# A planner's figures for loads and four ranks are changed, and the order of a retention + gated MLP kernel is planned anew

## The chip, the cores and the metric

The kernel runs on one core of a Trainium2 chip. The metric is the device time of one execution in microseconds (us); lower is better. Every time here comes from runs of this kernel or from the trace of one profiled execution.

## The reference, cut to what matters

Inputs: `q`, `k`, `v` of shape (4 batches, 8 heads, 768 tokens, 64), all fp32, and the weights `w_val`, `w_out` (512x512) and `conv_w` (5x512) of a gated layer.

```python
for t in range(S):                                   # retention, per batch and head
    state = gamma * state + outer(k[t], v[t])
    y[t]  = scale * q[t] @ state
x    = y as (batch, 768, 512)
gate = sigmoid(causal depthwise conv of x, 5 taps)
out  = (gate * (x @ w_val)) @ w_out
```

## The kernel before

The tokens are cut into 6 chunks of 128; a chunk of one batch is a unit `g` (24 units, `g = 4*chunk + batch`). A unit's q, k (transposed), v and k (natural) lie in a 1 MiB tile `att`; there are 4 such buffers, so unit g+4 overwrites unit g. The weights come as 8 tiles `wst` of 0.5 MiB and are converted on chip: w0 to w3 are `w_val`, w4 to w7 `w_out`. fp32 accuracy in the large matmuls comes from splitting both operands into a high and a low part (`xh`/`xl`, `wvh`/`wvl`, `gvh`/`gvl`, `woh`/`wol`) and adding three products.

Steps, with the line on which they show in the profile of the kernel before (in the changed kernel every one of these lines is 10 further down):

- First chunk, units 0 to 3: `first_scores` (L379, PE, writes `sy`), `first_mask` (L411, DVE, `sy` to `u`), `first_y` (L456, PE, writes `ye`), `evac` (L519, DVE, to `x`), `round_x` (L529, ACT, `xh`), `rest_x` (L534, POOL, `xl`), and `first_state` (L423, PE, writes `z_ps`). A POOL step `decay` (L355) scales a unit's k or v in place ahead of its state. `first_pos` (L498) makes a table from `pos`; `y` of unit 0 can only be evacuated behind it.
- Later units: a `head` for unit 4 (scores L366 and half of the state, L423), then one `visit` per unit: `y_scores` (L439), state (L423), a small ACT copy `turn`, `y_state` (L439) and the scores of the next unit (L366). Visits consist of 64x64 matmuls, each of which the profile shows as two.
- Per chunk and group m of 128 channels: 4 conv taps on DVE (L610) behind a first on ACT (L608), a sigmoid, and a val tile of 12 matmuls of 128x512 (L625); then per batch an out tile of 12 such matmuls (L659), a copy on ACT (L670) and a store.
- `filler` (L689): dummy matmuls that the planner puts into idle time of PE ahead of the first val matmul; `warm_up` is the same at the start.

The order on each engine isn't written by hand: `plan` simulates the five engines with the cost of each step, always takes the free step with the lowest rank (worked out backwards from the due times of the PE steps), and records the instructions in that order. The due times come from the string `WORK` (p: pos, s: first scores, y: first y, z: first state, h: head, v: visit, w: load and convert a weight, V: val tile, O: out tile) and from the list `LOADS`, the order of the first loads on SP's queue. In `LOADS` q is q and transposed k of a unit (0.5 MiB), v and k the other two (0.25 MiB each), a is q, k and v together (0.75 MiB), t the small table (68 KB), w a weight tile (0.5 MiB). Each engine runs its own instructions strictly in the recorded order.

Of the kernel before, what the change touches and what calls it, by code (L numbers as in the profile page):

```python
# [33 lines left out]
INTO, OUT_OF = 0.3, 0.134  # L34
COLD, WARM_AT = 1.85, 5.0
FIRST_PAGE, PAGE, FETCH, CROWDED = 94, 127.5, 3.0, 2.9
FIRST_BYTE, PER_MB = 4.1, 2.7
TABLES = (5.2, 9.3)

TIMES = {  # L40
# [6 lines left out]
}  # L47
FILL, FILLED = 0.46, 0.55
SEEN = {"DVE": 0.035, "ACT": 0.035, "POOL": 0.08, "PE": 0.08}


class Slot:
# [26 lines left out]
def plan(steps, filler, last, into):  # L79
# [5 lines left out]
    steps = sorted(steps, key=lambda s: s.due)  # L85
# [47 lines left out]
    while ends:  # L133
        t = ends.pop()
        for s in before[t.index]:
            if s.engine == "PE" or not hasattr(s, "rank"):
                s.rank = min(getattr(s, "rank", s.due if s.engine == "PE" else 1e9), 1e9)
            lag = s.cost + SEEN.get(t.engine, 0.0) if t in s.then else 0.0
            s.rank = min(s.rank, t.rank - lag) if s.engine != "DMA" else s.due
            left[s.index] -= 1  # L140
            if not left[s.index]:
                ends.append(s)
    clock, free = {}, {}

    def offer(s):
# [48 lines left out]
    def offered(e):  # L194
        return free[e] if e != "PE" or held is None else [s for s in free[e] if s is held]

    def done(s, end):
# [7 lines left out]
        for t in s.then:  # L205
            if t.engine == s.engine and not t.other:
                t.own = max(t.own, clock["PE"] if t.engine == "PE" else end + 0.03)
            else:
                t.ready = max(t.ready, end + SEEN.get(t.engine, 0.0))
            t.waits.discard(s.index)  # L210
# [3 lines left out]
    while any(free.values()):  # L214
# [5 lines left out]
        s = min(  # L220
            (s for s in offered(e) if max(s.ready, s.own if s.engine == e else 0.0) <= start),
            key=lambda s: (s.rank, s.index),
        )
# [26 lines left out]
        if s.turn:  # L250

            t, e = s.turn, s.turn.engine
# [10 lines left out]
def tile_retention_gated_mlp(  # L263
# [9 lines left out]
    nc = tc.nc  # L273
# [20 lines left out]
    small_sb = const.tile([P, small.shape[1]], F32, name="small_sb")  # L294
# [23 lines left out]
    steps = []  # L318

    def at(due, engine, cost, reads, writes, fn, *args):  # L320
        steps.append(Step(due, engine, cost, list(reads), list(writes), fn, args))
        return steps[-1]
# [371 lines left out]
    def first_sigmoid():  # L694
# [6 lines left out]


    CONV_LEAD, CHUNK = 7.0, 3.4
    LOADS = (("q", 0), ("t", 0), ("k", 0), ("v", 0), ("w", 0), ("a", 1), ("w", 1), ("a", 2), ("a", 3), ("k", 1), ("w", 2), ("k", 2), ("k", 3), ("w", 3))


    WORK = (
        "spysysszyyzzzVwwVwwhvVVOOvvOvOVvVvVVOvOvVVO"
        "vvVOvVvOVVOvOvVVOvvOVOvVOOvvvVVOVOOVVOVOOOO"
    )  # L710

    first_val = []
# [4 lines left out]
    def load_part_at(due, g, first, last):  # L717

        keys = [("att", g % LB, k) for k, part in (("qk", 0), ("vk", 2), ("kn", 3)) if first <= part < last]
        at(due, "DMA", 0.4, [], keys, load, g, slice(first, last)).mb = 0.25 * (last - first)  # L720
# [101 lines left out]
    def load_w_at(t, n):  # L822
        at(t, "DMA", 0.4, [], [wsts[n]], load_w, n).mb = 0.5
# [59 lines left out]
    at(0.2, "DVE", 0.25, [], [xbufs[0]] + [("x", 0, i) for i in range(B)], new_x, 0)  # L883
    for p, (kind, n) in enumerate(LOADS):
        t = 0.1 * p
        if kind == "t":
            at(t, "DMA", 0.4, [], ["small"], get, small_sb, small, nc.sync).mb = 0.2
        elif kind in "aqvk":
            load_part_at(t, n, *{"a": (0, 3), "q": (0, 2), "v": (2, 3), "k": (3, 4)}[kind])
        else:  # L890
            load_w_at(t, n)
    for x in range(2):
        for k, (engine, cost) in enumerate((("DVE", (0.42, 0.35)), ("ACT", (0.25, 0.2)))):
# [4 lines left out]
            )  # L898
    early = [n for kind, n in LOADS if kind == "w"]
    for n in ["cw"] + early:  # L900
        convert(5.5, n)

    t, whole = 6.0, {}
# [3 lines left out]
    for what in WORK:  # L907
# [7 lines left out]
        elif what == "s":  # L915
            t = max(t, 6.0 + CHUNK * i)
# [29 lines left out]
    with tc.manual_schedule():  # L946
        for step in plan(steps, filler, first_val[0], ("ye", "sc")):
            step.fn(*step.args)
# [93 lines left out]
```

## Time and profile before

| | |
|---|---|
| median of 3 runs | 210.98 us (210.53 to 211.2) |
| the profiled execution | 210.8 us |
| its span, first to last instruction | 209.0 us |
| granted TensorE clock | 1.00 |
| PE, DVE, ACT, POOL busy | 96%, 59%, 53%, 51% of the span |

In a row of the timeline stand the start, the length, the engine (PE is the matmul side of TensorE, SPq and ACTq are queues that issue DMAs), the line, the operation with what it writes and reads, the count, and in brackets the idle time of the engine before it and what ended that. Rows are merged runs of like instructions; matmuls are pipelined, so a row's length overlaps the next row, and differences of starts are used for durations. In a row of the windows view stand the stretch, its length, the busy time and number of instructions of each engine named, the clock, the DMA engines' busy share and their GB/s.

### The profile page before, as it was taken

The numbers are of one execution on the slowest core, as the hardware profiler recorded it, in microseconds if no ns is written. First come the engines' busy times: TensorE is split into PE (matmuls) and PEld (weight loads), VectorE is DVE, ScalarE is ACT, GpSimd is POOL, SyncE is SP. The second block draws the span as 40 slices with busy tenths as digits, with TensorE's granted clock in tenths as the row PEclk, the third lists the DMA queues.
The fourth block names the chain that finished last, engine by engine and source line by source line (L and its number), as shares of the span: only waits on it lengthen the run. The fifth ranks groups of instructions, "written<-read, shape, count | busy, mean of one in ns | idle before, by whom it ended". The sixth has DMA issues, their size and how long they took to land.

```text
span 209.0 us, 7837 instructions
## 1 busy us (share of the span) xinstructions
PE 199.7 (96%) x3502; PEld 159.3 (76%) x3502; DVE 123.5 (59%) x189; ACT 110.2 (53%) x237; POOL 105.9 (51%) x93
## 2 busy tenths in 40 slices
PE   8967898999999999999999999999999999999994
PEld 3647676788888888788887888788787788878783
DVE  1586999952399814899129992227796259921100
ACT  3584687774667434685338654146364445413121
POOL 0189999999824582536627324526142353204200
PEclk9999999999999999999999999999999999999999
DMA  6999994557555508527275138348111100120122
GB/s 213 411 408 412 418 413 167 204 172 274 167 204 204 204 3 279 226 94 258 109 256 204 50 108 270 130 161 299 53 50 53 56 0 0 50 103 0 50 100 102
DMA packets 9253, 36.24 MB, mean 173 GB/s; under 512 B 1154, under 2 KB 1538, under 8 KB 6660
## 3 DMA queue, kind: packets, MB, share of 16 engines
q1 hardware_dynamic: 5472, 29.43, 37.7%
q10 hardware_dynamic: 3748, 6.32, 8.2%
q8 instruction: 27, 0.44, 0.9%
q14 instruction: 6, 0.05, 0.1%
HBM read 29.46 MB, written 6.29 MB: 171 GB/s over the span
## 4 chain that ended last, share of the span: by engine, by line
PE 89%; DMA 7%; issue 1%; DVE 1%; SPq 0%; ACT 0%; ACTq 0%
PE mm L659 33%; PE mm L625 33%; PE sy L439 11%; PE z_ps L423 5%; DMA att<-in_att_dram 5%; PE sy L366 5%; DMA cw_raw<-in_conv_w_dram 2%; PE sy L689 1%; PE sy L379 0%; DVE u L411 0%; PE ye L456 0%; DVE x L519 0%; SPq L342 0%; ACT gate L670 0%; SPq L545 0%
## 5 line engine op out<-in xcount | busy, mean ns | idle before, releaser
L610 DVE SCALAR_TENSOR_TENSOR acc<-x,cw_sb,acc 128x512 f32<-128x512 f32 x96 | 66.8, 750 | 2.7 <-ACT acc L608 2.1
L534 POOL TENSOR_TENSOR xl<-x,xh 128x512 fp32r<-128x512 f32 x24 | 30.9, 1288 | 44.0 <-ACT xh L529 44.0
L651 POOL TENSOR_TENSOR gvl<-gate,gvh 128x512 fp32r<-128x512 f32 x24 | 30.9, 1289 | 30.6 <-ACT gvh L647 30.6
L659 PE MATMUL mm<-woh,gvl 128*128 128x512 f32 (+1 forms) x100 | 38.7, 396 | 0.0
L659 PE MATMUL mm<-woh,gvh 128*128 128x512 f32 (+1 forms) x100 | 38.2, 390 | 0.0
L659 PE MATMUL mm<-wol,gvh 128*128 128x512 f32 (+1 forms) x100 | 37.9, 387 | 0.0
L625 PE MATMUL mm<-xl,wvh 128*128 128x512 f32 x96 | 34.4, 399 | 0.0
L625 PE MATMUL mm<-xh,wvh 128*128 128x512 f32 x96 | 32.0, 399 | 0.0
L355 POOL TENSOR_TENSOR att<-att,small_sb 128x512 f32<-128x512 f32 x24 | 25.1, 1049 | 12.4 <-DMA att<-in_att_dram 12.4
L640 DVE TENSOR_TENSOR gate<-mm,gate 128x512 f32<-128x512 f32 x24 | 16.5, 688 | 20.5 <-PE mm L625 18.1
L625 PE MATMUL mm<-xh,wvl 128*128 128x512 f32 x96 | 27.0, 397 | 0.0
L647 ACT CAST gvh<-gate 128x512 fp32r<-128x512 f32 x24 | 14.9, 619 | 22.1 <-DVE gate L640 22.0
L388 DVE TENSOR_TENSOR u<-sy,small_sb 128x512 f32<-128x512 f32 x20 | 13.7, 687 | 21.6 <-PE sy L366 21.6
L519 DVE TENSOR_TENSOR x<-sy,dec 128x512 f32<-128x512 f32 x20 | 13.7, 683 | 17.3 <-PE sy L366 12.5
L659 PEld LDWEIGHTS mm<-woh,gvl 128*128 128x128 f32 x100 | 18.7, 188 | 4.7 <-POOL gvl L651 0.5
L670 ACT COPY o_sb<-mm 128x512 f32<-128x512 f32 x23 | 13.5, 586 | 16.5 <-PE mm L659 16.1
L659 PEld LDWEIGHTS mm<-woh,gvh 128*128 128x128 f32 x100 | 18.7, 188 | 4.4 <-ACT o_sb L670 0.2
L617 ACT ACTIVATE gate<-acc 128x512 f32<-128x512 f32 x24 | 14.4, 600 | 14.1 <-DVE acc L610 7.8
L529 ACT CAST xh<-x 128x512 fp32r<-128x512 f32 x24 | 14.9, 619 | 13.0 <-DVE x L519 12.1
L659 PEld LDWEIGHTS mm<-wol,gvh 128*128 128x128 f32 x100 | 18.7, 188 | 3.8
L625 PEld LDWEIGHTS mm<-xl,wvh 128*128 128x128 f32 x96 | 18.0, 188 | 4.4
L625 PEld LDWEIGHTS mm<-xh,wvl 128*128 128x128 f32 x96 | 17.9, 188 | 4.3
(52 smaller groups left out, 248.2 us busy)
## 6 DMA issues: line engine op xcount, KB each, us to landing
att<-in_att_dram SPq DMA_DIRECT2D x20, 1024.0 KB, 5.3
out_dram<-o_sb ACTq DMA_DIRECT2D x23, 256.0 KB, 2.2
wst<-in_w_dram SPq DMA_DIRECT2D x8, 512.0 KB, 8.7
att<-in_att_dram SPq DMA_DIRECT2D x3, 768.0 KB, 7.2
att<-in_att_dram SPq DMA_DIRECT2D x5, 256.0 KB, 10.4
att<-in_att_dram SPq DMA_DIRECT2D x1, 512.0 KB, 3.6
out_dram<-gate ACTq DMA_DIRECT2D x2, 128.0 KB, 1.7
small_sb<-in_small_dram SPq DMA_DIRECT2D x1, 68.0 KB, 3.5
```

Source lines behind the costliest of these rows:

```text
L355: nc.gpsimd.tensor_tensor(v, v, vd_sb[:, c, :].unsqueeze(2).broadcast_to([P, 8, HALF]), op=ALU.mult)
L388: nc.vector.tensor_tensor(us[g], sy[:, :, 0:256].rearrange("p x (a t) -> p x a t", t=HALF), tri_sb.unsqueeze(1).unsqueeze(1).broadcast_to( ...
L439: nc.tensor.matmul(sy[cols, h, off:off + HALF], lhsT=lhsT, rhs=rhs, start=start, stop=True, skip_group_check=True,)
L529: nc.scalar.copy(xh[n][:, :, b], xs[n][:, :, b, HALO:])
L534: nc.gpsimd.tensor_tensor(xl[n][:, :, b], xs[n][:, :, b, HALO:], xh[n][:, :, b].bitcast(F32), op=ALU.subtract)
L610: nc.vector.scalar_tensor_tensor(acc, x[:, :, k:k + P], cw_sb[:, m, k:k + 1], acc, op0=ALU.mult, op1=ALU.add,)
L617: nc.scalar.activation(gate[n, m], accs.pop((n, m)), AF.Sigmoid)
L625: nc.tensor.matmul(vps[n, m], lhsT=w[:, m, ct * P:(ct + 1) * P], rhs=xx[n][:, ct].rearrange("p b t -> p (b t)"), start=(i == 0), stop=(i = ...
L640: nc.vector.tensor_tensor(gv, vps.pop((n, m)), gv, op=ALU.mult)
L647: nc.scalar.copy(gvs[n, m][0], gate[n, m])
L651: engine.tensor_tensor(gvl, gate.pop((n, m)), gvh.bitcast(F32), op=ALU.subtract)
L659: nc.tensor.matmul(ops[n, b, cs.start][:, 0:cs.stop - cs.start], lhsT=gg[:, b * P:(b + 1) * P], rhs=w[:, ct, cs], start=(i == 0), stop=(i ...
```

## The change

Two figures of the planner for loads are changed (`FIRST_BYTE` and `PER_MB`, used for when a load lands), the size that it books for the small table goes from 0.2 to 0.13 MB, four kinds of steps get a number added to their rank (`LATER`: the split of unit 1 of the first chunk, the first state of unit 3, the sums of weights 3 and the rounding of weight 6), and `LOADS` and `WORK` are other sequences of the same steps. No step is added to the arithmetic or taken from it; the fillers, which `plan` places by itself, go from 11 calls to 13.

```diff
-FIRST_BYTE, PER_MB = 4.1, 2.7
+FIRST_BYTE, PER_MB = 3.0, 2.65
+LATER = {
+    ("rest_x", 0, 1): 1.47,
+    ("first_state", 3): -2.94,
...
+    for s in steps:
+        s.rank += LATER.get((s.fn.__name__, *(a for a in s.args if isinstance(a, int))), 0.0)
...
-    LOADS = (("q", 0), ("t", 0), ("k", 0), ("v", 0), ("w", 0), ("a", 1), ("w", 1), ("a", 2), ("a", 3), ("k", 1), ("w", 2), ("k", 2), ("k", 3), ("w", 3))
+    LOADS = (("q", 0), ("k", 0), ("t", 0), ("v", 0), ("a", 1), ("k", 1), ("w", 0), ("k", 2), ("k", 3), ("w", 1), ("a", 2), ("w", 2), ("a", 3), ("w", 3))
...
-        "spysysszyyzzzVwwVwwhvVVOOvvOvOVvVvVVOvOvVVO"
+        "sspyysyzszhyVVwzzwvVwvwVOOOvvvOVvvVVVvOVvOvV"
...
-            at(t, "DMA", 0.4, [], ["small"], get, small_sb, small, nc.sync).mb = 0.2
+            at(t, "DMA", 0.4, [], ["small"], get, small_sb, small, nc.sync).mb = 0.13
```

**SP's queue, the first loads.** A row is one load; 128x1024 is 0.5 MiB, x512 0.25, x1536 0.75, x2048 1 MiB. Before, from the second load on (`att_102` is unit 0, `att_120`, `att_126` and `att_129` are units 1, 2 and 3, `att_206` is unit 4):

```order
L342 DMA att_102<-in_att_dram 128x512 x2
L545 DMA wst_117<-in_w64_dram 128x1024
L342 DMA att_120<-in_att_dram 128x1536
L545 DMA wst_123<-in_w64_dram 128x1024
L342 DMA att_126<-in_att_dram 128x1536
L342 DMA att_129<-in_att_dram 128x1536
L342 DMA att_120<-in_att_dram 128x512
L545 DMA wst_133<-in_w64_dram 128x1024
L342 DMA att_126<-in_att_dram 128x512
L342 DMA att_129<-in_att_dram 128x512
L545 DMA wst_154<-in_w64_dram 128x1024
L342 DMA att_206<-in_att_dram 128x2048
```

After, where `att_116`, `att_125`, `att_128` and `att_245` are units 1, 2, 3 and 4:

```order
L352 DMA att_103<-in_att_dram 128x512
L352 DMA att_116<-in_att_dram 128x1536
L352 DMA att_116<-in_att_dram 128x512
L555 DMA wst_122<-in_w64_dram 128x1024
L352 DMA att_125<-in_att_dram 128x512
L352 DMA att_128<-in_att_dram 128x512
L555 DMA wst_131<-in_w64_dram 128x1024
L352 DMA att_125<-in_att_dram 128x1536
L555 DMA wst_150<-in_w64_dram 128x1024
L352 DMA att_128<-in_att_dram 128x1536
L555 DMA wst_157<-in_w64_dram 128x1024
L352 DMA att_245<-in_att_dram 128x2048
```

The natural k of units 1, 2 and 3 now comes ahead of q, k, v of units 2 and 3, and so does the third weight tile ahead of those of unit 3; the sum of bytes up to unit 4 is the same. On ACT's own queue, which loads the conv weights `cw_raw` and `pos`, the load of the sigmoid's table now stands ahead of these two instead of behind them.

**PE, from the y of unit 3 to the first val tile.** Before (`z_ps<-att_120`, `att_126`, `att_129` are the first states of units 1, 2, 3; `sy<-const` are filler calls):

```order
L456 MATMUL ye_96<-u_336,att_129 64x64 x8
L689 MATMUL sy_95<-const-float32-0.0 128x128 x2
L423 MATMUL z_ps_94<-att_120 64x64 x16
L689 MATMUL sy_95<-const-float32-0.0 128x128 x4
L423 MATMUL z_ps_94<-att_126 64x64 x16
L625 MATMUL mm_428<-xh_217,wvh_89 128x512 x4
L423 MATMUL z_ps_94<-att_129 64x64 x16
L625 MATMUL mm_428<-xh_217,wvl_90 128x512 x4
```

After (`sy<-att_245` and `z_ps<-att_245` are the head of unit 4):

```order
L466 MATMUL ye_96<-u_365,att_128 64x64 x8
L699 MATMUL sy_95<-const-float32-0.0 128x128 x6
L376 MATMUL sy_95<-att_245 64x64 x16
L433 MATMUL z_ps_94<-att_245 64x64 x8
L635 MATMUL mm_447<-xh_272,wvh_89 128x512 x4
L635 MATMUL mm_447<-xh_272,wvl_90 128x512 x4
```

Three fillers and the head now stand ahead of the first val matmul; the first state of unit 1 has moved up to the loads' first stretch, and those of units 2 and 3 behind it. On POOL, which feeds this, stood before:

```order
L355 TENSOR_TENSOR att_120<-att_120,small_sb_86 128x512
L534 TENSOR_TENSOR xl_242<-x_104,xh_217 128x4x128
L355 TENSOR_TENSOR att_126<-att_126,small_sb_86 128x512
L355 TENSOR_TENSOR att_129<-att_129,small_sb_86 128x512
L534 TENSOR_TENSOR xl_242<-x_104,xh_217 128x4x128
L582 TENSOR_TENSOR top_341<-top_341,up_342 128x512
```

and stands now:

```order
L544 TENSOR_TENSOR xl_280<-x_105,xh_272 128x4x128
L365 TENSOR_TENSOR att_245<-att_245,small_sb_86 128x512
L592 TENSOR_TENSOR top_362<-top_362,up_363 128x512
L544 TENSOR_TENSOR xl_280<-x_105,xh_272 128x4x128
L365 TENSOR_TENSOR att_282<-att_282,small_sb_86 128x512
```

The decays of units 1 to 3 (`att_120`, `att_126`, `att_129` before) have moved to the front of POOL's order; now the decay of unit 4 and the sum of the third weight tile stand ahead of the split `xl` of unit 3, which is the last `xl` row of each list.

**PE, ahead of the first visit.** Before, head and first visit (`u_559`) with 12 val matmuls between them:

```order
L366 MATMUL sy_95<-att_206 64x64 x16
L423 MATMUL z_ps_94<-att_206 64x64 x8
L625 MATMUL mm_536<-xh_217,wvh_89 128x512 x4
L625 MATMUL mm_536<-xh_217,wvl_90 128x512 x4
L625 MATMUL mm_536<-xl_242,wvh_89 128x512
L625 MATMUL mm_561<-xh_217,wvh_89 128x512
L625 MATMUL mm_536<-xl_242,wvh_89 128x512
L625 MATMUL mm_561<-xh_217,wvh_89 128x512
L439 MATMUL sy_95<-u_559,att_206 64x64 x16
```

After, with the first states of units 2 and 3 (`att_125`, `att_128`) and three val matmuls ahead of the first visit (`u_480`):

```order
L635 MATMUL mm_465<-xh_272,wvl_90 128x512 x4
L635 MATMUL mm_465<-xl_280,wvh_89 128x512
L433 MATMUL z_ps_94<-att_125 64x64 x16
L433 MATMUL z_ps_94<-att_128 64x64 x16
L635 MATMUL mm_465<-xl_280,wvh_89 128x512 x3
L449 MATMUL sy_95<-u_480,att_245 64x64 x16
```

Small matmuls now stand closer together there: three val matmuls lie between the states and the visit instead of twelve between head and visit. On all of PE the changed order has 22 separate runs of large matmuls, the order before 23.

More of the change, by code (lines that the diff above doesn't have):

```diff
@@ L49 @@
 SEEN = {"DVE": 0.035, "ACT": 0.035, "POOL": 0.08, "PE": 0.08}
+LATER = {
+    ("rest_x", 0, 1): 1.47,
+    ("first_state", 3): -2.94,
+    ("cv_sum", 3): 0.77,
+    ("cv_round", 6): 3.83,
+}
 class Slot:
@@ L703, in tile_retention_gated_mlp @@
     CONV_LEAD, CHUNK = 7.0, 3.4
-    LOADS = (("q", 0), ("t", 0), ("k", 0), ("v", 0), ("w", 0), ("a", 1), ("w", 1), ("a", 2), ("a", 3), ("k", 1), ("w", 2), ("k", 2), ("k", 3), ("w", 3))
+    LOADS = (("q", 0), ("k", 0), ("t", 0), ("v", 0), ("a", 1), ("k", 1), ("w", 0), ("k", 2), ("k", 3), ("w", 1), ("a", 2), ("w", 2), ("a", 3), ("w", 3))
     WORK = (
-        "spysysszyyzzzVwwVwwhvVVOOvvOvOVvVvVVOvOvVVO"
-        "vvVOvVvOVVOvOvVVOvvOVOvVOOvvvVVOVOOVVOVOOOO"
+        "sspyysyzszhyVVwzzwvVwvwVOOOvvvOVvvVVVvOVOvV"
+        "vVvVvOvOVOOvVVVvvOOVOVvVvvOvVOOVVOOOVOVOOOO"
     )
```

## The prediction

> **What bounds the kernel now.** I read the page first, then PE's time by stretches.
>
> ```profile
> PE 199.7 (96%) x3502; PEld 159.3 (76%) x3502; DVE 123.5 (59%) x189; ACT 110.2 (53%) x237; POOL 105.9 (51%) x93
> q8 instruction: 27, 0.44, 0.9%
> ```
>
> ```profile
> 40.00:80.00 40.00, 40.00 (x881) 1.00 0.47 168
> 80.00:120.00 40.00, 40.00 (x765) 1.00 0.52 185
> ```
>
> From 40 us on PE has no gap; DVE, ACT and POOL have half of their time free. Both orders hold the same 588 large matmuls and the same visits, so whatever the change does to the middle moves nothing unless it opens a gap there. The time is decided by how soon the first val matmul starts, what is left to do by then, and the gaps around the first visit. PE's timeline there:
>
> ```profile
> 15.75 1.00 PE L379 MATMUL sy<-att 64*64 64x128 f32 x32 [0.76 <-DMA att<-in_att_dram]
> 18.43 0.90 PE L456 MATMUL ye<-u,att 64*64 64x128 f32 x32 [1.01 <-DVE x L519]
> 19.25 0.71 PE L689 MATMUL sy<-const-float32-0.0 128*128 128x128 f32 x4
> 22.12 0.71 PE L689 MATMUL sy<-const-float32-0.0 128*128 128x128 f32 x5 [1.00 <-issue]
> 22.77 0.69 PE L423 MATMUL z_ps<-att 64*64 64x64 f32 x32
> 23.39 1.20 PE L625 MATMUL mm<-xh,wvh 128*128 128x512 f32 x4
> 24.52 0.69 PE L423 MATMUL z_ps<-att 64*64 64x64 f32 x32
> 25.15 1.20 PE L625 MATMUL mm<-xh,wvl 128*128 128x512 f32 x4
> 30.01 0.69 PE L366 MATMUL sy<-att 64*64 64x64 f32 x32
> 30.52 0.41 PE L423 MATMUL z_ps<-att 64*64 64x64 f32 x16
> 30.87 1.20 PE L625 MATMUL mm<-xh,wvh 128*128 128x512 f32 x4
> 33.86 0.69 PE L439 MATMUL sy<-u,att 64*64 64x64 f32 x32
> 36.29 0.68 PE L366 MATMUL sy<-att 64*64 64x64 f32 x27 [0.66 <-issue]
> ```
>
> The scores of unit 3 wait for their load (15.75), the first val matmul starts at 23.39, the first visit at 33.86. Two waits are put down to "issue", to no other engine and no tensor's load. They stand 255 matmuls apart by the order (254 recorded, first row below). The page counts 27 packets on the instruction queue for 3502 matmuls and as many weight loads, 130 matmuls a packet, so two packets lie between the waits. I read them as PE's own code arriving late.
>
> ```profile
> 22.12:36.28 14.16, 13.51 (x254) 1.00 0.82 333
> 136.57:140.34 3.77, 3.77 (x142) 1.00 0.44 148
> 65.72:67.78 2.06, 2.06 (x130) 1.00 0.41 167
> 33.86:36.90 3.04, 2.38 (x130) 1.00 0.16 35
> 5.20:31.00 25.80, 21.41 (x480) 16.48 (x480) 20.10 (x32) 17.70 (x38) 20.99 (x19) 1.00 1.02 412
> ```
>
> If a block is asked for when the one before it begins, the block that arrived at 36.29 was asked for 127 matmuls after 22.12, at the head's state (30.5): 5.8 us, while loads filled the DMA engines (share 1.02 until 31). In a calm stretch 142 matmuls ran in 3.77 us without a wait, so a block then takes 3.8 us at most. The first visit cost 3.04 us against 2.06 for a common one: 1.0 lost.
>
> **The start, part by part.** *Loads.* SP's queue has new places, but through unit 3's q, k, v it now carries as many bytes (5.57 MiB) as it did through the natural k of unit 3, and through unit 4 the same 7.07 MiB. Those two landed at 7.6 + 11.3 = 18.9 and 11.0 + 11.7 = 22.7:
>
> ```profile
> L342 SPq DMA_DIRECT2D att<-in_att_dram x1: 328/328/328, 7.6 to 7.6; - x1
> DMA to landing us min/median/max: 11.3/11.3/11.3
> L342 SPq DMA_DIRECT2D att<-in_att_dram x1: 328/328/328, 11.0 to 11.0; - x1
> DMA to landing us min/median/max: 11.7/11.7/11.7
> ```
>
> With the DMA engines full throughout (412 GB/s), I take the same times. So unit 3 comes 3.2 us later than before (15.7), unit 4 when it did. The natural k's come some 6 us earlier by the same count; their three decays move to POOL's idle first stretch, off the path.
>
> *First val matmul.* From the rows below: mask 1.07 after its scores start, 0.96 long; y at once.
>
> ```profile
> 16.82 0.96 DVE L411 TENSOR_TENSOR u<-sy,xh 128x768 f32<-128x768 f32 x1 [1.71 <-PE sy L379]
> 20.81 0.67 ACT L608 ACTIVATE acc<-x,cw_sb 128x512 f32<-128x512 f32 x1
> 21.42 0.60 ACT L529 CAST xh<-x 128x512 fp32r<-128x512 f32 x1
> 18.70 1.05 POOL L355 TENSOR_TENSOR att<-att,small_sb 128x512 f32<-128x512 f32 x1
> 22.93 1.30 POOL L534 TENSOR_TENSOR xl<-x,xh 128x512 fp32r<-128x512 f32 x1
> 24.17 2.55 POOL L582 TENSOR_TENSOR top<-top,up 128x512 int32<-128x512 int32 x2
> ```
>
> Scores 19.0, mask 20.1 to 21.0, y 21.1 to 21.9 (as 18.43 to 19.25). Then six filler calls, 12 rows; five took 0.65 (22.12 to 22.77), some of it the change to other matmuls, so 1.5. Head at 23.4, its state at 23.9 (30.01 to 30.52), val 0.35 later: 24.3. Two other paths end with it. POOL decays unit 4 from 22.8 to 23.9, just in time for that state. And the y of unit 3 goes to `x` behind two weight steps on DVE (22.3 to 22.9), then a first tap (0.67) and `xh` (0.60) on ACT: 24.2. Against 23.39, 0.9 later. Then POOL: behind the decay stand a weight sum (1.28) and the last `xl` (1.30), so `xl` is there at 26.5; the ninth val matmul wants it at 24.3 + 8 x 0.233 = 26.2: wait 0.3.
>
> *What is left.* From the first val matmul to the first visit there now stand 21 + 3 val matmuls and two states: 5.1 (20 took 25.15 to 30.01) + 2 x 0.63 + 0.9 (12 took 2.99 behind 30.87) = 7.25. The visit starts at 24.3 + 0.3 + 7.25 = 31.85. Before, it started at 33.86 with 12 more val matmuls done (2.8), so the place to compare is 31.05: 0.8 behind.
>
> *First visit.* By the order, one block of code now begins in the state of unit 3 and the next in that visit's scores; between them lie half a state, three val matmuls and most of a visit, 0.3 + 0.9 + 1.7 = 2.9 us, where before it was 5 (30.5 to 35.5). So PE waits between 0 and 5.8 - 2.9 = 2.9. The load of unit 6 decides. Its buffer is freed by the state of unit 2, now at 29.7; before, such a load was issued at 25.32 behind a state at 24.52, 0.8 later:
>
> ```profile
> 25.32 0.33 SPq L342 DMA_DIRECT2D att<-in_att_dram  x1
> 35.62 0.33 SPq L342 DMA_DIRECT2D att<-in_att_dram  x1
> ```
>
> So it goes at 30.5; the code is asked for at 30.7, when the loads before it (10.07 MiB by then, 2.5 us per MiB behind 22.7) have landed at 30.2. The engines are empty just then, nearest to the calm row; I take 0.3, for a block of some 3.2 us (the calm row's 3.8 is only an upper bound), and 0.1 for the next, which has 5.8 us. So 1.0 lost becomes 0.4.
>
> *What costs nothing.* The other changed ranks sit on POOL and ACT; from 40 us on their slack covers them. In the first visit mask and tap work ends at 29.6 by my count, 2 us ahead of it; if that cover went, each us late would be a us. The sigmoid's table now loads on ACT ahead of `cw_raw` and `pos`, 1.5 us; `pos` is wanted behind unit 1's scores, at 9 us. The last 58 out matmuls and the final store keep their order.
>
> *Sum:* +0.8 - 1.0 + 0.4 = +0.2 on the profiled execution's 210.8 us (span 209.0), 211.0; the median of the runs is 0.2 above that execution: 211.2.
>
> **A rule against the trace.** The Trainium skill, "Runtime: NRT & Kernel Launch", section "Instruction fetch mechanics", says that each engine's code is refilled in 16 KiB blocks and that crossing a boundary is mostly hidden. The 27 packets of 0.44 MB fit the block size; the waits of 1.00 and 0.66 don't fit the hiding. By the rule the first visit would wait for nothing, and the sum would be -0.2 instead of +0.2.
>
> **Rivals.**
> - *Slower: the code comes behind unit 6's load.* The request and that load's issue are 0.2 us apart. If the load's packets are first, the block takes 5.8 and PE waits 2.9, the next block perhaps 0.2: 211.2 + 2.6 = 213.8, and half of it if only some packets are ahead. It decides once a block takes over 3.7. For it: 36.29, where it happened with loads in flight; against it: the load's first bytes must come before the request. The Trainium skill, "DMA: Bandwidth & Descriptors", section "Queues, rings and completion order", has each DMA engine go round its queues packet by packet, which would keep such a delay short; 5.8 us against 3.8 at most says that this trace doesn't bear that out.
> - *Faster: the start fits better.* Unit 4's landing plus decay and state hold the first val matmul at 24.1 at least. With that, no wait for `xl` and no wait for code, it is +0.3 - 1.0 = -0.7: 210.3. For it: three paths end within 0.4 us; against it: all three must be early.
> - *Slower: a gap in the loads.* Before, the first load that needs a free lane of SP's queue waited for `cw_raw` to land (first row below). Now the natural k of unit 2 stands there in the order, and ACT issues `cw_raw` 1.5 us later; if it landed past 9 us, the loads would run dry, and each us moves units 3 and 4 by one: +1, 212.2. Against it: `cw_raw` took 3.8 us from issue to landing (second row), which makes 6.1.
>
> ```profile
> SPq L545 <- DMA cw_raw<-in_conv_w_dram: 1.0, 1, 1.0
> ...
> 0.73 3.79 DMA cw_raw<-in_conv_w_dram
> ```
>
> **How the numbers follow.** 0.3% (0.63 us) is about what a measurement of this kernel can tell from no change. The forecast, 211.2 (210.6 to 211.7 with the bounds of the small terms), gets 0.45; code behind the load 0.30, of which nearly all is slower by more than 0.63; the better start 0.17; the gap in the loads 0.08. So faster 0.17, same 0.45, slower 0.38. The range reaches from the better start, 210.3, to 213.5, leaving out the worst of the code case.
>
> **What would show it.** Right: unit 3's scores start near 19.0, the first val matmul near 24.3 with the head just ahead, the ninth waits some 0.3 on POOL, the first visit takes 2.2 to 2.6 us. Wrong: an "issue" wait of over a us in the first visit, a first val matmul before 23.8 or after 25, or gaps on PE behind 45 us, where I expect none.

## Result and profile after

The changed kernel takes 212.56 us in the median of 10 runs (211.57 to 214.31), the kernel before 210.98 (210.53 to 211.20). The ratio is 1.0071 with a 95% interval of 1.0048 to 1.0095: slower by 0.7%. The profiled execution is the fastest of the ten, 211.57 us with a span of 209.8. So two things have to be found: the 0.77 us between the two profiled executions, and the 1.0 us that a middling run has on top.

The page's first lines, after:

```profile
span 209.8 us, 7834 instructions
PE 201.3 (96%) x3506; PEld 159.9 (76%) x3506; DVE 125.1 (60%) x189; ACT 110.1 (52%) x237; POOL 106.1 (51%) x93
q8 instruction: 27, 0.44, 0.8%
```

PE is 1.6 us busier in a span 0.8 longer. PE's timeline, after, from unit 2's scores to the second visit (start, duration, line, matmuls, in brackets the idle time ahead and its releaser):

```profile
15.90 0.90 PE L389 MATMUL sy<-att 64*64 64x128 f32 x32 [1.36 <-DMA att<-in_att_dram]
19.07 0.90 PE L389 MATMUL sy<-att 64*64 64x128 f32 x32 [0.28 <-DMA att<-in_att_dram]
21.87 1.60 PE L699 MATMUL sy<-const-float32-0.0 128*128 128x128 f32 x12
23.41 0.69 PE L376 MATMUL sy<-att 64*64 64x64 f32 x32
24.37 1.20 PE L635 MATMUL mm<-xh,wvh 128*128 128x512 f32 x4
29.72 1.16 PE L433 MATMUL z_ps<-att 64*64 64x64 f32 x64
30.81 0.96 PE L635 MATMUL mm<-xl,wvh 128*128 128x512 f32 x3
31.71 0.69 PE L449 MATMUL sy<-u,att 64*64 64x64 f32 x32
33.19 1.05 PE L376 MATMUL sy<-att 64*64 64x64 f32 x32
34.17 1.19 PE L635 MATMUL mm<-xh,wvh 128*128 128x512 f32 x4
38.09 0.69 PE L449 MATMUL sy<-u,att 64*64 64x64 f32 x32
```

Scores of unit 3 at 19.07, head at 23.41, first val matmul at 24.37, first visit from 31.71 to 34.17. With the 12 val matmuls (2.80) that the kernel before had done by its first visit, the place is 34.51 against 33.86: 0.65 behind. The first visit took 2.46 instead of 3.04. So far that is +0.07. The rest came where I had expected nothing. Last matmuls, before and then after:

```profile
205.62 0.27 PE L659 MATMUL mm<-woh,gvl 128*128 128x256 f32 x1
206.50 0.27 PE L669 MATMUL mm<-woh,gvl 128*128 128x256 f32 x1
```

and the 18 visits from the third on, each from its first small matmul to the next large one, summed (first number), before and then after:

```profile
sum 36.77, PE 36.37 PEld 34.61 DVE 10.91 ACT 18.84 POOL 20.16; mean PE 2.02 PEld 1.92 DVE 0.61 ACT 1.05 POOL 1.12
sum 37.18, PE 36.62 PEld 34.85 DVE 14.53 ACT 20.71 POOL 26.53; mean PE 2.03 PEld 1.94 DVE 0.81 ACT 1.15 POOL 1.47
```

The end is 0.88 later: 0.65 at the start, -0.58 in the first visit, +0.13 in the second (2.40 against 2.27), +0.41 in the other 18, and the remaining 0.27 between visits.

The trace shows where the 0.41 sits. In each visit PE's `y_state` follows the small ACT copy `turned`. In 10 of these 18 visits, against 3 before, that copy starts 0.80 to 0.82 us after the visit's first matmul instead of 0.76 or 0.77, and the visit is about 0.05 longer: seven more such visits make the 0.4. Two copies of the changed kernel, in the visits that start at 55.68 (2.06 long) and 67.04 (2.12):

```profile
56.44 0.16 ACT L499 COPY turned<-sy 64x2 f32<-64x2 f32 x1 [0.43 <-PE sy L449]
67.86 0.15 ACT L499 COPY turned<-sy 64x2 f32<-64x2 f32 x1 [0.22 <-PE sy L449]
```

ACT was idle ahead of both, waiting for PE; why the copy starts later in some visits stays open.

### The profile page after: what moved, and what is told of

Read it like the earlier page. It is cut to its first block, busy times and chain, and to the rows that moved or that the text cites. A ratio compares the mean times of both kernels' runs of the same rounds, so it can differ in the third digit from the quotient of the medians.

```text
span 209.8 us, 7834 instructions
## 1 busy us (share of the span) xinstructions
PE 201.3 (96%) x3506; PEld 159.9 (76%) x3506; DVE 125.1 (60%) x189; ACT 110.1 (52%) x237; POOL 106.1 (51%) x93
## 4 chain that ended last, share of the span: by engine, by line
PE 89%; DMA 8%; SPq 1%; DVE 0%; issue 0%; ACT 0%; ACTq 0%
PE mm L635 33%; PE mm L669 33%; PE sy L449 12%; DMA att<-in_att_dram 8%; PE sy L376 5%; PE z_ps L433 4%; PE sy L699 1%; SPq L352 1%; DVE u L421 0%; PE sy L389 0%; PE ye L466 0%; ACT turned L499 0%; SPq L355 0%; ACT gate L680 0%; ACTq L499 0%
## 5 line engine op out<-in xcount | busy, mean ns | idle before, releaser
L620 DVE SCALAR_TENSOR_TENSOR acc<-x,cw_sb,acc 128x512 f32<-128x512 f32 x96 | 67.9, 752 | 7.1 <-ACT acc L618 6.2
L669 PE MATMUL mm<-woh,gvl 128*128 128x512 f32 (+1 forms) x100 | 37.9, 392 | 0.0
L669 PE MATMUL mm<-woh,gvh 128*128 128x512 f32 (+1 forms) x100 | 37.6, 390 | 0.0
L635 PE MATMUL mm<-xh,wvh 128*128 128x512 f32 x96 | 32.8, 397 | 0.0
L635 PEld LDWEIGHTS mm<-xh,wvh 128*128 128x128 f32 x96 | 17.9, 188 | 4.0
```

Of the source, the lines that this page charges most:

```text
L620: nc.vector.scalar_tensor_tensor(acc, x[:, :, k:k + P], cw_sb[:, m, k:k + 1], acc, op0=ALU.mult, op1=ALU.add,)
L635: nc.tensor.matmul(vps[n, m], lhsT=w[:, m, ct * P:(ct + 1) * P], rhs=xx[n][:, ct].rearrange("p b t -> p (b t)"), start=(i == 0), stop=(i = ...
L669: nc.tensor.matmul(ops[n, b, cs.start][:, 0:cs.stop - cs.start], lhsT=gg[:, b * P:(b + 1) * P], rhs=w[:, ct, cs], start=(i == 0), stop=(i ...
```

## Experiments

All kernels below edit the list of steps that the planner returns, or numbers that it is given; the diffs are cut to what they do. `filler` is the program's own dummy matmul; `shift("sc", n)` stands for n small matmuls of zeros (64 rows, 64 columns) into columns 384 to 448 of the score bank, which nobody reads. That a block of code is asked for when the one ahead of it begins is inferred, as in the prediction; no row shows a request. A fall is a stretch in which the granted clock stood at 0.50. The first theory was the rival of the prediction: the block of PE's code that is asked for at 30.5 races with unit 6's load, issued at 30.51, wins in the fast run and loses in the others.

**e1, code blocks 40 rows earlier.** `last` is the three filler calls ahead of the head.

```diff
+order[last[1]].fn, order[last[1]].args = shift, ("sc", 24)
+del order[last[2]]
```

> The changed kernel; of the six filler matmuls ahead of the head four are replaced by 24 small matmuls of zeros (64 rows, 64 columns) into an unused part of the score bank. TensorE works through its code in blocks, so 40 more rows bring every later block boundary 40 rows earlier: the boundary that fell in the second of the two states ahead of the first visit (30.48 us, 0.03 before unit 6's load was issued) now falls early in the first of them, about 0.6 us before that load. Theory A (the 1 us between the profiled run and the median, and the spread, are a race of that block's request with unit 6's load): no late block, first visit under 2.6 us, median 211.3 to 211.7 and runs within 0.6 of each other. Theory B (the spread comes from when loads and decays land, not from code): median stays at 212.3 to 212.8 and runs spread over 2 us as before.

Measured: 214.01 us (213.20 to 214.16), 1.0143 [1.0122, 1.0164] of before. In the profile the first visit starts at 31.85 and takes 2.36, as theory A had it, and the kernel is slower all the same. Code came late elsewhere, behind the twelfth visit and in the thirteenth:

```profile
106.72 0.50 PE L669 MATMUL mm<-woh,gvl 128*128 128x512 f32 x1 [0.86 <-issue]
111.43 0.39 PE L376 MATMUL sy<-att 64*64 64x64 f32 x10 [0.36 <-issue]
```

40 rows move every later boundary too. Against the changed kernel's first profile, e1 is 0.52 us behind at its twelfth visit and 2.25 at its fourteenth, of 2.35 at the last matmul. Clearing one place by shifting the code pays at another. (In three of the four runs the clock fell as well, of which more below.)

**e2, code blocks 16 rows later.** `drop` is the filler ahead of the head and ahead of unit 2's scores.

```diff
+for i in reversed(drop):
+    del order[i]
```

> The changed kernel without the six filler matmuls ahead of the head and without the filler ahead of unit 2's first scores: 16 rows fewer, so the boundary that raced with unit 6's load falls some 0.4 us after that load was issued. Theory A (race with the load): the block comes late in every run, as 3.2 to 3.8 us from boundary to packet did elsewhere in these traces with loads in flight; TensorE waits 2 to 3.5 us inside the first visit, in the row of its scores or of its second y half, and the median is 213.3 to 214.6 with a narrow spread. Theory B (no race; spread from loads and decays): unchanged, 212.3 to 212.8, or up to 0.3 better if filler delays real work. A lower clock from the missing filler would show in the granted clock of the first 40 us.

Measured: 212.53 us (212.12 to 213.57), 1.0086 [1.0065, 1.0107]. The loss of 2 to 3.5 us that the race should have brought in every run is not there; the first visit took 2.80 (31.99 to 34.79). Theory A falls as I put it. The mean clock was 0.992 or less in all six runs, as the expectation allowed for with filler gone, and the median is the changed kernel's all the same.

**e3, the two states ahead of the first visit swapped.**

```diff
+i, j = place(first_state, 2), place(first_state, 3)
+order[i], order[j] = order[j], order[i]
```

Where unit 6's load stood ahead of unit 2's state in the list, it was put behind it.

> The changed kernel with the two states ahead of the first visit in the other order (unit 2's first, then unit 3's), so that unit 6's load, which waits for unit 2's... state to be read, is issued at another time than the block's boundary while the code's blocks lie where they lay: if unit 2's state going first frees the buffer 0.5 us sooner, the load is issued before the boundary; if it goes later, after it. Read the order off the profile first. Theory A (race of the request with this load): the boundary ahead of the load gives 211.3 to 211.7 and a narrow spread; the boundary behind it gives a wait of 2 us or more in the first visit and 213 or more. Theory B (landing of unit 6's load itself): a load that is issued 0.5 us later costs up to 0.5 us, one issued sooner gains up to 0.5, and the spread of 2 us stays.

Measured: 212.15 us (211.43 to 214.59), 1.0069 [1.0040, 1.0097]. The load that was to move was issued at 30.46, 0.05 from where it was, so the run set up neither case. It counts as one more run of nearly the same order: same spread.

**e5, the kernel before with unit 4's scores early and 40 rows more.**

```diff
+order[i].fn, order[i].args = state, (LB, 0)          # i: the head
+order.insert(j + 1, Step(0, "PE", 0, [], [], scores, (LB,)))   # j: unit 3's first state
+order[idle[1]].fn, order[idle[1]].args = shift, ("sc", 22)
```

> The kernel before; the scores of unit 4 are taken out of the head and stand right behind unit 3's first state, some 5 us earlier, and one filler call ahead of unit 2's first state is replaced by 22 small matmuls of zeros, 40 rows more. The block boundary that fell at the head's state (30.54 us) now falls in these scores (about 25.7), so the block in which the first visit ends is asked for 4.8 us sooner; the boundary behind it falls in the first visit at about 34.7, 0.9 us before unit 8's load is issued. Theory A (the first visit's 3.03 us in the kernel before are 1 us of late code): the visit takes 2.1 us, the end comes 0.9 to 1.0 us sooner, median 209.9 to 210.2. Theory B (the visit is long for something else, such as the mask or the snapshot of the unit): it stays at 3.0 us and the time at 210.8 to 211.1.

Measured: 216.52 us (215.05 to 217.40), 1.0262 [1.0232, 1.0293]; I had it faster.

```profile
22.58 0.27 PE L689 MATMUL sy<-const-float32-0.0 128*128 128x128 f32 x1 [0.51 <-issue]
28.87 0.56 PE L366 MATMUL sy<-att 64*64 64x64 f32 x18 [2.73 <-issue]
43.36 0.47 PE L659 MATMUL mm<-woh,gvh 128*128 128x512 f32 x1 [1.04 <-DVE gate L640]
```

I had looked only at the block behind the moved boundary. The block in front of it had been asked for at the boundary before, at 22.58, and came 6.3 us later; PE reached it after 3.6 us and stood 2.73. The first visit itself took 2.07, as expected. Of the 6.1 us that this execution is longer, 4.1 are there at the second visit (45.38 against 41.27), another 0.6 at the last matmul, and 1.4 come behind it: the last store went out at 211.11 and the span ended at 215.1, before at 206.39 and 209.0.

**again_1 and again_2, the changed kernel, unaltered, for two more profiled executions.**

> The changed kernel once more, unaltered, for a second profiled execution: the first was 211.57 us and the fastest of its runs (median 212.56, up to 214.31). Theory A (late code blocks at places that change from execution to execution, since a block asked for while a load is on its way takes 5.7 to 6.2 us and otherwise 3.0 to 3.7): the start is the same to 0.2 us (first visit at 31.6 to 31.9), and what an execution has above 211.57 stands in single visits or stretches between them, 0.3 to 1.1 each, with TensorE waiting for nothing that the profile shows. Theory B (landings of the first loads differ): the surplus is there already when the first visit begins, and every later visit is the same length.

> The changed kernel a third time, unaltered; as for the second: theory A puts the surplus over 211.57 in single later visits (0.3 to 1.1 each), theory B into the start of the first visit, by more than 0.3 later than 31.71.

Measured: 214.24 and 212.76 us. The table is worked out from PE's timelines: start and length of the first visit, the second with the val matmuls behind it, the stretch behind the fourth visit, the sixth visit; `clock` is the run's mean granted clock.

```
run             us    clock  1st visit at, length  2nd+behind  behind 4th  6th
after         211.57  1.000     31.71    2.46         5.84        5.49    2.06
again_2       212.76  0.992     31.94    2.37         5.91        5.81    2.66
again_1       214.24  0.984     32.77    2.65         6.12        5.35    3.16
g1_gap_filled 211.51  1.000     31.54    2.07         6.42        5.32    2.06
g2_gap_wider  213.68  0.992     32.57    2.72         6.12        5.32    2.78
```

Both theories are half right: again_1 has 1.06 of its 2.67 at the start of the first visit and 1.10 in the sixth, again_2 has 0.23 and 0.60. What the start lost is the clock: unit 2's scores start at 15.88 in again_1 and 15.72 in again_2, no later than the 15.90 of the first profile, so the loads up to there weren't late. By stretches of 1 us (width, then busy time of PE, its weight load, DVE, ACT and POOL with instructions, then the granted clock), of again_1:

```profile
15.00:16.00 1.00, 0.12 (x4) 0.12 (x8) 0.70 (x2) 1.00 (x4) 0.97 (x2) 0.76 1.05 434
16.00:17.00 1.00, 1.00 (x24) 1.00 (x28) 0.00 (x0) 1.00 (x4) 1.00 (x1) 0.50 0.95 387
21.00:22.00 1.00, 1.00 (x14) 0.67 (x6) 0.57 (x1) 1.00 (x3) 0.43 (x1) 0.50 1.00 418
22.00:23.00 1.00, 1.00 (x25) 0.56 (x26) 0.99 (x2) 0.62 (x2) 0.97 (x2) 0.83 1.03 426
```

and in the changed kernel's first profile:

```profile
16.00:17.00 1.00, 1.00 (x33) 0.93 (x34) 0.40 (x2) 1.00 (x3) 0.96 (x2) 1.00 1.00 408
```

The clock stood at half from 15.52 (0.48 of that us) to 22.34: 6.8 us. In again_2 the same count gives 17.56 to 20.98, 3.4 us, so the steps are 3.4 long. In the 3.41 us ahead of the fall PE had been busy for 1.78 and 1.60 (second number; again_1, then again_2):

```profile
12.11:15.52 3.41, 1.78 (x39) 1.33 (x37) 3.29 (x6) 3.41 (x9) 3.02 (x4) 1.00 1.02 411
14.15:17.56 3.41, 1.60 (x35) 1.06 (x34) 2.58 (x4) 3.39 (x10) 3.38 (x4) 1.00 1.01 413
```

The wait there is the one for unit 2's load: 1.36 us in the first profile, 1.82 and 1.50 in these. In e1, e2 and e3 it was 1.50, 2.68 and 1.66, and one fall came at the same place. The first visit was late by 1.06 us behind the two steps of again_1, and by -0.05 to 0.28 behind the single steps of again_2, e1, e2 and e3. The Trainium skill, "TensorE: Matmul & The Clock Gate", section "What's actually happening", has the clock at half after an idle window of about 3.4 us, in windows that run free of the kernel. The length of the falls agrees, and free windows would explain why the same order falls in one execution and not in another; but here PE was busy for half of the stretch, not idle. Nor does the busy share of the 3.41 us ahead decide it by itself. The profile of g2, below, fell after 2.62 busy us (first row), e5 stayed at 1.00 (second row) although PE stood for 2.73 us there, and figures_alone stayed there through a wait of 1.82:

```profile
8.03:11.44 3.41, 2.62 (x71) 1.68 (x70) 0.69 (x2) 0.65 (x2) 1.14 (x2) 1.00 1.03 410
27.00:28.00 1.00, 0.00 (x0) 0.00 (x0) 0.04 (x1) 0.97 (x3) 1.00 (x2) 1.00 0.95 385
```

What the sixth visit lost is a second thing: ACT. Of again_1, ACT's timeline, then PE's:

```profile
60.27 0.59 ACT L680 COPY o_sb<-mm 128x512 f32<-128x512 f32 x1 [2.27 <-DMA out_dram<-o_sb]
66.24 0.69 PE L449 MATMUL sy<-att,snap 64*64 64x64 f32 x32 [0.90 <-ACT turned L499]
```

The first store of an output tile landed 6.4 us after its issue at 53.84 (in the first profile 4.0 us after 52.43), ACT waited for its buffer, everything behind that copy on ACT came late, and the sixth visit waited for `turned`. In again_2 ACT waited 1.62, in g2 1.73; in the other profiles of this order (g1, e1, e2, e3) not at all. The three profiles with the wait all had a fall, but so had e1, e2 and e3 without it; whether a fall makes the store late wasn't tested.

**old_loads, the changed kernel with the order of the first loads as before.**

```diff
-LOADS = (("q", 0), ("k", 0), ("t", 0), ("v", 0), ("a", 1), ("k", 1), ("w", 0), ...
+LOADS = (("q", 0), ("t", 0), ("k", 0), ("v", 0), ("w", 0), ("a", 1), ("w", 1), ...
```

> The changed kernel with the order of the first loads as before (its new step string, ranks and planner figures kept; the planner then sets the steps of the other engines anew). As before it has 24 val matmuls ahead of the first visit, and unit 3's load comes in as one of three parts. If the new order of loads is what makes the start late (unit 3's load at 18.9 us, +0.7 at the first visit): a first visit about 0.5 to 0.7 sooner against work done, 211.0 to 211.9. If the start is late through the order of the steps: no sooner, 212 or more, since loads and steps were made for one another. Late code: its block boundary falls in the first of the two states (about 29.5), ahead of unit 6's load, so no wait over 0.5 in the first visit by theory A.

Measured: 215.39 us (213.72 to 216.32), 1.0204 [1.0156, 1.0253]. Undoing one part alone is far worse: with 24 val matmuls ahead, as in the changed kernel, the first visit starts at 34.75 instead of 31.71. The clock stood at half from 12.4 to 19.2 there, and all four runs had a mean clock under 0.993, so how much is the order and how much the clock stays open.

**figures_alone, the kernel before with the planner's new figures.**

```diff
-FIRST_BYTE, PER_MB = 4.1, 2.7
+FIRST_BYTE, PER_MB = 3.0, 2.65
-at(t, "DMA", 0.4, [], ["small"], get, small_sb, small, nc.sync).mb = 0.2
+at(t, "DMA", 0.4, [], ["small"], get, small_sb, small, nc.sync).mb = 0.13
```

> The kernel before with the planner's figures for loads alone (3.0 us to the first byte and 2.65 us a megabyte, 0.13 MB for the small table); no new ranks, no new order. The planner believes loads sooner by 1.1 us than it did, so it sets fewer idle fillers (18 rows of them fewer) and a slightly other order of vector and gpsimd work. If the planner's wrong figures cost something before: 210.3 to 210.7. If such a plan, without the search, only moves code boundaries to other places: within 0.3 of 210.8 where they miss the loads, and 211.5 to 213.5 where one falls behind a load; its boundary ahead of the first visit falls in the head's scores (about 30.0), 0.5 sooner than before, so its first visit should lose 0.5 instead of 1.0.

Measured: 211.68 us (211.23 to 213.18), 1.0041 [1.0020, 1.0063]. With these figures alone the plan is slower. In the profiled execution, the slowest of the eight, the first visit took 2.15, so most of the late code was gone there, and out matmuls waited 0.63 for `gate` at 41.34 instead. Most of its loss was there earlier: the first visit starts at 35.74 instead of 33.86, behind waits of 1.68 and 1.82 us for loads.

**g1, two filler calls more in the idle stretch ahead of unit 2's scores.**

```diff
+order[i:i] = [Step(0, "PE", 0, [], [], filler, ("sc",)) for _ in range(2)]
```

> The changed kernel with two more filler calls (four matmuls of zeros) behind the one that stands ahead of unit 2's scores, where TensorE idles 1.36, 1.50 and 1.82 us for unit 2's load in its three profiled executions; the idle time falls to about 0.3. Theory A (the clock: after the longer idle stretches the granted clock stood at 0.50 for 3 to 7 us, 16 to 23 us from the start, and each such execution began its first visit 0.2 to 1.1 late): no granted clock under 1.00 in the first 30 us, first visit at 31.6 to 31.8, median 211.3 to 211.8, little above 212.2 in any run. Theory B (the clock's drop only goes along with late loads, which are what costs): the spread and the median of 212.5 stay.

Measured: 211.97 us (211.51 to 212.33), 1.0045 [1.0028, 1.0061]. The wait fell to 0.57:

```profile
15.62 0.90 PE L389 MATMUL sy<-att 64*64 64x128 f32 x32 [0.57 <-DMA att<-in_att_dram]
39.64 0.39 PE L449 MATMUL sy<-att,snap 64*64 64x64 f32 x10 [0.59 <-issue]
```

The mean clock was 0.998 or more in all 6 runs, where 7 of the changed kernel's 12 had 0.992 or less; the runs above 212.4, 8 of those 12, are gone. But the changed kernel's own five runs at full clock lie at 211.57 to 212.63 (median 212.48). So the falls go with the tail, all three runs over 213, and aren't the whole of the 1.0 us. The edit doesn't part the clock from the code either: the two calls add 8 rows of code, the first visit takes 2.07 instead of 2.46, and the second waits 0.59 as in the second row, put down to "issue" like late code. The two ratios' intervals overlap, too.

**g2, the idle stretch made wider.**

```diff
-filler("sc")
+shift("sc", 2)
```

> The changed kernel with the filler call ahead of unit 2's scores replaced by two small matmuls of zeros (as many rows of code), so that TensorE idles there some 0.5 us longer, 1.9 to 2.4 us. Theory A (the clock): the granted clock falls to 0.50 in nearly every execution and earlier (from about 15.5 us), the first visit begins at 32.3 to 33.0, median 213 to 214.3. Theory B (late loads, clock without effect): as the changed kernel, median 212.3 to 212.8.

Measured: 212.66 us (212.22 to 213.68), 1.0086 [1.0061, 1.0111]. All four runs had a clock of 0.992, one fall each, but the median is theory B's. In the profile the clock fell at 11.4, ahead of the stretch, and was back before it, and the wait came out at 0.46. So which stretch brings the fall isn't settled by width alone. With e2, ten runs that all fell have medians of 212.53 and 212.66, against 212.48 for the changed kernel's runs at full clock: a fall by itself costs the median little.

**g3, the kernel before with 40 more rows of code and nothing moved.**

```diff
+order[idle[1]].fn, order[idle[1]].args = shift, ("sc", 22)
```

> The kernel before with one of the filler calls ahead of unit 2's first state replaced by 22 small matmuls of zeros: 40 more rows behind the block boundary at 22.1 us and nothing moved. The boundary that fell in the head's state (30.54) now falls among the val matmuls at 28.5 to 28.7, just when the block asked for at 22.1 is there (28.3 to 28.9: 6.2 us later, as in the run that moved the scores); the next boundary falls in the first visit at about 34.8, and its block, asked for at 28.6, is there 5.7 to 6.2 us later, 34.3 to 34.8. Theory A (late code is the 0.98 us that the first visit loses in the kernel before): the visit takes 2.1 to 2.5, median 209.9 to 210.4, faster than both kernels. Rival: a block comes later than that or the next boundary falls behind unit 8's load (issued 35.6) and a wait of 0.5 to 1 stands elsewhere: 210.6 to 211.5.

Measured: 211.34 us (210.70 to 213.19), 1.0040 [1.0018, 1.0061].

```profile
33.61 0.69 PE L439 MATMUL sy<-u,att 64*64 64x64 f32 x32
35.67 0.51 PE L625 MATMUL mm<-xl,wvh 128*128 128x512 f32 x1
38.87 0.47 PE L659 MATMUL mm<-woh,gvh 128*128 128x512 f32 x1 [0.59 <-DVE gate L640]
```

The first visit takes 2.06, so the 0.98 that it has above that in the kernel before is late code. But removing it bought almost nothing. In the profile g3 is 1.23 us ahead at the end of the first visit (35.67 against 36.90), 0.37 at the second, behind a wait of the out matmuls for `gate` on DVE, and 0.09 at the last matmul. The late block had been hiding a wait that was next in line.

**h1, the kernel before with its early filler taken out and its rows of code kept.**

```diff
-filler("sc"), filler("ye"), filler("ye"), filler("sc")
+shift("sc", 3), shift("sc", 3)
```

> The kernel before with its four filler calls between unit 0's y and unit 1's state (8.7 to 20 us) taken out and six small matmuls of zeros in their place, as many rows of code, so that every code block begins where it did; only TensorE's idle time between 8 and 20 us grows, by about 2.4 us. Theory A (the clock: where TensorE was busy for about half of a stretch of 3.4 us, the granted clock then stood at 0.50 for one or two stretches of 3.4 us, in the changed kernel's start, and that is what its median has above its fastest run): the granted clock now falls here too, the first visit begins 0.2 to 1.1 later than 33.86 in the profile, median 211.3 to 212.5 and a spread of over 1 us. Theory B (loads and landings set the start, the clock goes along with them): 210.8 to 211.2 as before, with or without a fall of the clock.

Measured: 211.44 us (211.10 to 212.59), 1.0031 [1.0006, 1.0056], as theory A had it. All 12 runs fell, against 7 of 59 runs of the unaltered kernel beside these experiments. They order themselves by the number of 3.4 us steps at half clock, which the mean clock counts: one (0.992) 211.10 to 211.19 in five runs, two (0.984) 211.41 and 211.47, three (0.976) 212.03 to 212.59 in five. Its profile, with one step: PE busy 7.71 us (first number behind the width) of 8 to 20 us, before 8.66, and the first visit at 34.37 instead of 33.86.

```profile
8.00:20.00 12.00, 7.71 (x266) 6.88 (x256) 8.46 (x14) 9.32 (x22) 8.39 (x8) 0.86 1.03 412
8.00:20.00 12.00, 8.66 (x240) 6.91 (x244) 8.91 (x15) 9.03 (x21) 8.95 (x9) 1.00 1.03 414
```

One step costs little, where PE waits for loads anyway; three cost a microsecond.

No kernel beat the kernel before.

## Why the prediction came out as it did

The range held the time and the likeliest case didn't: 211.2 was forecast, 212.56 came. That the range held is luck in part: its part above 211.7 stands for the rivals "code behind unit 6's load" and "gap in the loads", and neither happened. By its steps:

- *Loads and first val matmul: right.* Unit 3's scores at 19.07 (forecast 19.0), head at 23.41 (23.4), first val matmul at 24.37 (24.3).
- *What is left: right.* First visit at 31.71 (31.85), 0.65 behind (0.8). The wait for `xl` was about 0.15 (0.3).
- *First visit: nearly right.* It lost 0.40 (0.3) and the next 0.34 (0.1). In the kernel before, g3 and e5 showed the wait to be PE's code: with the boundary moved the visit took 2.06 and 2.07. In e5 a block took 6.3 us with loads in flight, where I had 5.8.
- *"Moves nothing unless it opens a gap there": wrong.* This is the step that failed in the sum. The visits from the third on took 0.41 more and the stretches between 0.27, with no new gap among PE's waits: +0.68 of the +0.88. The 0.41 comes from `turned`, which starts 0.05 later in seven more visits than before; why it does, and where the 0.27 lies, stays open.
- *The profiled execution taken for the runs: wrong.* I added 0.2 for the median. The change turned a kernel whose runs lie within 0.7 us into one whose runs lie within 2.7 (of 59 later runs of the kernel before one took 213.20, the others at most 211.66). Nothing in the profile of before showed that the clock could fall, and I did not ask what PE's longer wait for unit 2's load (1.36 against 0.76) would do to it. The three runs above 213 all had a fall, but the falls explain little of the median (7 fallen runs 212.77, 5 at full clock 212.48, all twelve 212.63). The late store takes 0.6 to 1.1 more in those profiles in which it happened. How much of the full-clock runs' 0.9 over the fastest is the store, and how much the second visit and the stretch behind the fourth, which vary by up to 0.6 and 0.5 between the profiles, stays open: only one full-clock execution of this kernel was profiled.
- *Rival "code behind unit 6's load": didn't happen.* In eight profiles of this order the first visit took 2.07 to 2.80, never 2.9 us more. e2, with the request later, took 2.80.
- *Rival "gap in the loads": its premise was false.* ACT issued `cw_raw` at 0.80, against 0.73 before, and it landed 3.5 us later (and 0.73 + 1.5 + 3.8 would have made 6.0, not 6.1):

```profile
L355 ACTq DMA_DIRECT2D cw_raw<-in_conv_w_dram x1: 386/386/386, 0.8 to 0.8; - x1
DMA to landing us min/median/max: 3.5/3.5/3.5
```

- *The rule on code fetches* (the Trainium skill, "Runtime: NRT & Kernel Launch", section "Instruction fetch mechanics": mostly hidden) gave -0.2 and no wait in the first visit. The 0.40 there and the 2.73 of e5 speak against it for dense small matmuls.

## What to carry to other kernels

Where TensorE is made to wait longer for a load, the wait's price is also what the granted clock may do behind it, and a kernel whose clock falls in some executions (7 of 12 here) is forecast from several of them, not from the one that was profiled. As e5 has it, a late code block was asked for one boundary earlier, so a boundary can only be moved if the block ahead of it is there too, and each shift moves all later ones. When a wait is removed, price the next one in line: g3 took away 0.98 us of waiting and ended 0.09 sooner.

## What the runs showed of the hardware

- The granted clock fell to 0.50 for whole steps of 3.4 us (one in again_2, two in again_1, up to three in h1) with PE busy for 0.73 us (e2) to 2.62 us (g2) of the 3.4 ahead. It did not fall in e5, where PE stood for 2.73 us. What decides it stays open.
- A block of PE's code took 6.3 us with loads in flight (22.58 to 28.87 in e5), if it was asked for when the block ahead of it began.
- One store of an output tile landed after 4.0 us in one execution and 6.4 in another of the same kernel, and the sixth visit took 1.1 longer behind it.
